# Twenty loads of r and w moved from SP's queue to ScalarE's in a two-phase recurrence and mixing kernel

## The chip, the cores and the metric

The kernel runs on one core of a Trainium2 chip. The metric is the time of one execution on the device, in microseconds (us); each time shown is the median of a few executions. The profile is one further execution, taken by the hardware profiler.

## The reference

Two phases follow each other. The first is a recurrence over 768 steps for 4 batches and 8 heads of width 40, the second mixes its output over tokens and over channels.

```python
for t in range(S):                                   # S = 768, state is [B, H, D, D]
    y[:, :, t] = einsum('bhd,bhde->bhe', rt, state)
    Sa = einsum('bhde,bhe->bhd', state, at)
    state = state * wt[:, :, None, :] - einsum('bhd,bhe->bhde', Sa, bt) \
            + einsum('bhd,bhe->bhde', vt, kt)
x = y.transpose(0, 2, 1, 3).reshape(B, S, H * D)
theta = x @ w_theta
zr, zi = x * cos(theta), x * sin(theta)
u = x + einsum('ts,bsd->btd', w_tok_r, zr) + einsum('ts,bsd->btd', w_tok_i, zi)
out = u + maximum(u @ w_ch, 0)
```

All inputs and the output are float32.

## The kernel before

The 768 steps of a batch are cut into six chunks of 128, so there are 24 tiles (four batches of six), numbered 0 to 23. Within a tile the recurrence is written as matrix products: decays from sums of log w, masked score matrices, a small carried state. A tile needs six inputs of 128 x 8 x 40 floats (160 KB): r, k, v, w, a, b. For r and w one load brings two tiles at once (320 KB), so an even tile's load serves the odd tile behind it as well.

What is done when is written out by hand. The string `ORDER` is a list of some 1,400 entries such as `LDR:4`, `LN:6A` or `PSI:4@1`: a step's name, the tile, for some the engine (A is ScalarE, ACT in the profile; V is VectorE, DVE; G is GpSimd, POOL; S is SyncE, SP) and the PSUM bank. A loop at the end runs through it and calls one function an entry. Each engine gets its instructions in the written order and runs them one after the other, waiting on semaphores where an operand or a buffer is not ready. The entries that this text speaks of:

- `LDW`, `LDR`, `LDK`, `LDB`, `LDA`, `LDV`: the loads of w, r, k, b, a, v (L348, L334, L354 for k and b, L359 for a and v). All are issued by SP's queue. `raw_w` and `raw_r` have three buffers each, the others five.
- `LDT`: a load of rows of a token-mixing weight (`wtok_raw`, L773), also SP's; `ST` stores a tile of the output; a few transposes are SP's DMAs too.
- `LN:i`: ScalarE's logarithm of w for tiles i and i+1 (`lw_two`, L366). The sums, `INVW` (L401) and `WI` (L443) on ScalarE, and `KH` and `AH` on POOL come from it.
- `CR:i`: the cast of r for two tiles (`r`), on ScalarE or POOL.
- ScalarE's many other entries move or cast results out of PSUM (L293), and TensorE's next products wait for these: `EGD` (`gd`), `EPHI` (`phi`), `ERT` (`rvT`), `ETH` (`th`) among them; `SIN` is the sine and cosine with a table load before it (L728).

Each hardware DMA reports its landing on one of eight completion semaphores, `DMAHW0` to `DMAHW7` in the rows below, with 16 for a whole load. The recording layer gives them out in turn, in the order in which it places the DMAs, and a DMA first waits until every earlier one on its semaphore has landed.

Of the kernel before, what the change touches and what calls it, by code (L numbers as in the profile page):

```python
# [19 lines left out]
LDW:2 LDW:0 LDK:0 LDA:1 LDC:0.0G LDC:0.2G LDA:0 LN:0A LDB:0 CSE:0@0 CSI:0@1 LN:2A CST:0 LDB:1  # L20
LDK:1 INVW:0A WI:0A LDK:2 AH:0V CSI:2@1 CSE:2@0 AH:1V KH:0V CST:2 LDB:2 TRA:0@0 TRK:0@3 LDV:0
EAT:0A INVW:2A LDR:0 EKBT:0V LDA:2 WI:2A KH:1V PHI:0@1 EPHI:0A PSI:0@0 LDV:1 KH:2G TRA:1@2
EPSI:0V TRK:1@1 EKBT:1V LDB:3 CV:0A MPHI:0G EAT:1A X0:0@0 TRK:2@3 EKBT:2V LDK:3 ENX:0A CR:0A
PHI:1@1 PSI:1@0 EPHI:1V LDV:2 AH:2G TRV:0@2 EPSI:1A TRR:0@1 NU:0 LDW:4 EVT:0V ENU:0A TRA:2@3
MPSI:1G GT:0@0 CV:1A EAT:2V EGT:0V ERT:0A NUT:0@2 LDR:2 PSI:2@0 ENUT:0A PHI:2@1 EPSI:2A TRV:1@3
EPHI:2V KH:3G X0:1@0 LDA:3 ENX:1A LDB:4 LV:0@0 NU:1 EVT:1A LU:0@1 CV:2G ENU:1A ELV:0V TRK:3@2
MPSI:2G ELU:0A NUT:1@3 LDK:4 ERT:1V GT:1@0 GI:1 ENUT:1V LN:4A LV:1@0 LU:1@1 MLU:0G EGT:1V
TRV:2@1 LDV:3 X0:2@3 CR:2G ELV:1A Y:0@0 ELU:1V ENX:2A CSI:4@0 LDA:4 AH:3G LDB:5 EX:0V CSE:4@1
INVW:4A EKBT:3V CST:4 MLV:1G TRA:3@0 LDK:5 WI:4A TRR:2@2 EAT:3V NU:2 EVT:2A ERT:2V KH:4G PSI:3@0
EPSI:3V PHI:3@1 ENU:2A ERT:3A GD:0@0 GT:2@1 LDR:4 NUT:2@3 EGD:0A GI:2 ENUT:2V EPHI:3A LDW:6  # L30
TRK:4@2 AH:4G EGT:2V LU:2@0 EKBT:4V CV:3A LV:2@1 MPHI:3G LDA:5 X0:3@0 ELU:2A TRA:4@3 Y:1@1
ELV:2V MLU:2G ENX:3A NU:3 EAT:4V TRV:3@2 LDV:4 ENU:3A LDK:6 EX:1V GD:1@3 PHI:4@0 EVT:3V KH:5G
PSI:4@1 EGD:1A GT:3@0 EPSI:4A EPHI:4V NUT:3@1 Y:2@2 CR:4G ENUT:3V LN:6A LV:3@0 LDB:6 EX:2V
LU:3@1 ELU:3V TRK:5@3 MPSI:4G ELV:3A LDA:6 TRR:4@1 ERT:4A AH:5G GI:3 GD:2@2 EGT:3V CSE:6@0 LDV:5
CSI:6@1 EGD:2A EKBT:5V CV:4G INVW:6A TRA:5@0 LDK:7 MLV:3G X0:4@2 ENX:4A ERT:5V CST:6 EAT:5V
TRV:4@3 XT:1@1 LDB:7 WI:6A XT:0@0 EVT:4V NU:4 KH:6G LDR:6 PHI:5@1 EXT:1A EXT:0V PSI:5@0 ENU:4A
EPHI:5V TH:0@3 AH:6G EPSI:5A NUT:4@0 TRK:6@1 ENUT:4V LDW:8 EKBT:6V LV:4@1 MPSI:5G LU:4@0 Y:3@2
LDV:6 LDA:7 SIN:0A CV:5G ELU:4V GT:4@0 GI:4 TRV:5@1 KH:7G EGT:4V ELV:4A EVT:5V MLV:4G TH:1@3
X0:5@0 EX:3V XT:2@1 SIN:1A LDB:8 LV:5@0 TRA:6@2 ENX:5V EXT:2V ELV:5A GD:3@3 EAT:6V TH:2@1 NU:5
CR:6G SIN:2A EGD:3V MLV:5G PSI:6@1 PHI:6@0 LDA:8 ENU:5V EPSI:6V LDV:7 Y:4@2 NUT:5@3 LDK:8  # L40
TRR:6@0 ENUT:5V CV:6G EPHI:6V LN:8A TRK:7@1 X0:6@3 ENX:6A AH:7G LU:5@1 ZR:1G LDB:9 LDK:9 CSE:8@0
ERT:7A ELU:5V NU:6 CST:8 ERT:6A ENU:6A TRA:7@0 ZR:2G EKBT:7V WI:8A AH:8G LDW:10 CSI:8@1 EAT:7V
GD:4@3 INVW:8A TRV:6@1 EX:4V PSI:7@0 PHI:7@1 NUT:6@0 EVT:6V EPSI:7V LDA:9 GT:6@2 KH:8G EGD:4A
Y:5@1 LDV:8 EPHI:7A EGT:6V CV:7A LV:6@0 ENUT:6V MPHI:7G TRA:8@3 EAT:8A EX:5V LDT:0.0 X0:7@2
TRK:8@0 ENX:7V ELV:6A GD:6@1 XT:4@3 EKBT:8V KH:9G NU:7 LDT:0.1 ENU:7A LU:6@1 EXT:4V PSI:8@0
EGD:6V NUT:7@0 EPSI:8V XT:3@3 ELU:6A TRV:7@2 ZR:0G TRK:9@1 ENUT:7A LDV:9 LDR:8 EXT:3V LU:7@1
GT:7@0 AH:9G LN:10A TH:3@3 CV:8G LDK:10 EKBT:9V TH:4@1 ELU:7V GI:7 CW:0.0G PHI:8@0 SIN:3A EVT:7V
LDT:1.0 MLU:6G EGT:7V LV:7@1 SIN:4A TRA:9@2 XT:5@3 EXT:5A X0:8@0 EPHI:8V LDB:10 WT:0.0@1 EAT:9V
CW:0.1G ENX:8A EWT:0.0A ELV:7V TH:5@3 MLV:6G PSI:9@0 EPSI:9V SIN:5A WT:0.1@2 CR:8G NU:8 TRV:8@1
EVT:8V LDT:1.1 ENU:8A LDA:10 Y:7@3 EWT:0.1A CV:9G CSI:10@1 EX:7V PHI:9@0 GT:8@0 LDR:10 ZR:5G  # L50
CW:1.0G NUT:8@2 GI:8 LDV:10 EPHI:9V TRR:8@1 EGT:8V Y:6@3 INVW:10A CSE:10@0 KH:10G LDB:11 CST:10
ENUT:8A ERT:9A LDK:11 EX:6V ERT:8V X0:9@0 WT:1.0@3 WI:10A ENX:9V TRV:9@2 CW:1.1A EWT:1.0V LV:8@1
LU:8@0 AH:10G ELV:8V TRK:10@1 YR:0.0@3 EVT:9A LDT:2.0 ZR:3G NU:9 EKBT:10A CV:10G YR:0.1 TRA:10@2
LDW:12 LV:9@1 ELU:8V ENU:9A YR:0.2 ZR:4G EAT:10A GD:7@1 EGD:7A ELV:9V CR:10A WT:1.1@0 GT:9@2
LDA:11 GI:9 PSI:10@0 EPSI:10A EGT:9V PHI:10@1 EWT:1.1V EPHI:10V LDT:2.1 NUT:9@1 TRR:10@2 Y:8@0
ENUT:9A MPSI:10G ERT:10A TRV:10@1 EX:8V YR:0.3 YR:0.4 LDK:12 EVT:10V X0:10@0 LDB:12 KH:11G
ERT:11V LN:12A ENX:10V LV:10@0 LU:9@1 ELV:10A CW:2.0G YR:0.5 ELU:9V NU:10 LDV:11 TRK:11@1
ENU:10A GD:8@2 CW:2.1A AH:11G EU:0V LDA:12 EKBT:11V CSI:12@0 CSE:12@1 CST:12 LDW:14 TRA:11@0
WT:2.1@3 EAT:11V INVW:12A KH:12G WT:2.0@1 LDK:13 WI:12A LDB:13 PSI:11@0 EWT:2.1A EWT:2.0V
PHI:11@1 XT:6@0 EPSI:11V NUT:10@1 GT:10@3 EGD:8A CV:11A GI:10 Y:9@2 EXT:6A LDT:3.0 AH:12G  # L60
EPHI:11A MPHI:11G TRV:11@0 EGT:10V LDC:0.4G EX:9V TRK:12@3 ENUT:10V EKBT:12V EVT:11A MLV:10G
# [6 lines left out]
ELU:11V ZR:7G CSE:14@0 ERT:12A ERT:13V PSI:13@1 LDV:14 EX:10V CW:3.1A CST:14 TRV:12@2 EVT:12A
EPSI:13V YR:1.4 KH:14G LDR:14 YR:1.5 NU:12 WI:14A GD:10@1 WT:3.1@2 ENU:12V EGD:10A LDK:15
PHI:13@1 LV:12@0 EWT:3.1V GT:12@0 EU:1V CV:13G EPHI:13A NUT:12@1 ENUT:12A AH:14G EGT:12V  # L70
TRV:13@2 ELV:12V Y:11@3 LDB:15 TRK:14@0 EVT:13A MPHI:13G LDT:4.1 YR:3.0@1 EX:11V LV:13@1 ELV:13V
LU:12@0 EKBT:14A ZR:8G UT:0@2 TRA:14@3 EAT:14V X0:13@0 ELU:12A YR:3.1 LDT:4.0 YR:3.2 ENX:13A
YR:3.3 CV:14A CR:14A PHI:14@1 PSI:14@0 EUT:0A MLU:12G TRV:14@3 LDA:15 EPHI:14V YR:3.4 EVT:14A
NU:13 YR:3.5 EU:3V LDW:16 UT:1@2 ENU:13A KH:15G TRR:14@3 EUT:1A CW:4.1G NUT:13@0 ERT:14A CH:0@1
ENUT:13V CHR:1@2 CH:1 EPSI:14A LDV:15 EO:0V Y:12@0 CW:4.0G EO:1V LV:14@1 LU:13@0 ERT:15A EX:12V
ST:1 GD:12@1 EGD:12V XT:9@2 TRK:15@3 EXT:9V EKBT:15V GT:13@0 ELU:13A WT:4.1@1 EWT:4.1V TH:9@2
AH:15G ELV:14A MPSI:14G TRA:15@3 EAT:15V ST:0 MLU:13G GI:13 LDT:5.1 ETH:9A WT:4.0@1 XT:11@2
ZR:6G EGT:13V LN:16A PHI:15@0 EWT:4.0V LDT:5.0 PSI:15@1 X0:14@3 EXT:11V LDK:16 XT:10@0 CV:15G
YR:4.0@1 YR:4.1 ENX:14V TH:11@2 LDB:16 EXT:10V SIN:9A NU:14 EPHI:15V YR:4.2 ETH:11A LDA:16
ENU:14A TH:10@0 CW:5.1G YR:4.3 SIN:10A Y:13@2 EPSI:15V EX:13V GT:14@3 LDK:17 NUT:14@0 SIN:11A  # L80
ZR:10G CSI:16@0 CSE:16@1 EUT:2S EGA:14V EGT:14V CW:5.0G TRV:15@2 YR:4.4 EVT:15V YR:4.5 LDB:17
X0:15@3 ENUT:14V INVW:16A EU:4V CST:16 KH:16G WT:5.1@2 ENX:15V LDW:18 WI:16A WT:5.0@0 EWT:5.1V
LU:14@0 LV:15@1 EWT:5.0V ELV:15V NU:15 LDR:16 XT:12@1 YR:5.0@2 LDV:16 AH:16G YR:5.1 ELU:14A
ENU:15A TRK:16@0 LDA:17 MLU:14G TRA:16@3 EXT:12V EKBT:16V YR:5.2 YR:5.3 EAT:16A NUT:15@1 MLV:14G
UT:3@0 LDK:18 EUT:3V GD:13@3 EGD:13A PHI:16@0 KH:17G PSI:16@1 ENUT:15A EPHI:16V CH:2@0 YR:5.4
# [809 lines left out]
```

## Time and profile before

| | |
|---|---|
| median of 3 runs | 206.38 us (205.11 to 210.47) |
| profiled execution | 205.09 us |
| span from its first to its last instruction | 203.4 us |
| TensorE (PE) busy | 186.8 us, 92% |
| VectorE (DVE) busy | 169.8 us, 83% |
| ScalarE (ACT) busy | 150.1 us, 74% |
| GpSimd (POOL) busy | 148.1 us, 73% |
| hardware DMA queue, share of the 16 DMA engines | 83.9% |

An engine's busy time counts its own instructions; issuing a DMA or waiting on a semaphore is not in it. The 1.7 us between span and execution lie around the span. All sums in the prediction are made against the profiled execution.

### The profile page before, as it was taken

Reading aid. Unit: us, or ns where it says so; the run is one execution under the profiler, and the core shown is the slowest. Engines: PE = TensorE matmul, PEld = TensorE weight load, DVE = VectorE, ACT = ScalarE, POOL = GpSimd, SP = SyncE. Lnnn points to the kernel's source line nnn. Section 1 sums busy time; section 2 is a strip of 40 time slices with the busy share of each in tenths; the row PEclk is TensorE's granted clock in tenths of the full one; section 3 lists DMA queues with packets and bytes.
Section 4 is the critical chain, followed back from the end, with each engine's and each line's share of the span. In section 5 each row is a group of like instructions: output and inputs, shape, how many; then the busy total and the mean of one; then the engine's idle time right before and its main releaser. Section 6 shows DMA issues by size and latency. Waiting matters only on the chain.

```text
span 203.4 us, 7844 instructions
## 1 busy us (share of the span) xinstructions
PE 186.8 (92%) x3282; PEld 147.3 (72%) x3282; DVE 169.8 (83%) x324; ACT 150.1 (74%) x273; POOL 148.1 (73%) x155
## 2 busy tenths in 40 slices
...
GB/s 156 182 192 157 206 173 197 141 212 158 208 269 266 197 248 178 212 238 175 224 270 207 201 175 177 140 207 214 152 164 77 181 190 127 74 75 53 193 77 129
DMA packets 141955, 35.95 MB, mean 177 GB/s; under 512 B 136352, under 2 KB 140384, under 8 KB 141920
## 3 DMA queue, kind: packets, MB, share of 16 engines
q1 hardware_dynamic: 140864, 34.85, 83.9%
...
q14 instruction: 10, 0.08, 0.1%
HBM read 29.54 MB, written 3.93 MB: 165 GB/s over the span
## 4 chain that ended last, share of the span: by engine, by line
PE 68%; DVE 9%; ACT 8%; DMA 8%; POOL 3%; SPq 2%; issue 1%; POOLq 0%; DVEq 0%; ACTq 0%
PE sm L306 35%; PE sc L306 16%; PE sm L310 16%; DMA raw_kb<-in_b_dram 5%; DMA wtok_raw<-in_moe_w_tok_i_dram 3%; POOL kb L303 2%; DVE phi L303 1%; ACT cs L728 1%; DVE lamu L303 1%; DVE rvT L295 1%; SPq L359 1%; ACT rvT L293 1%; DVE kbT L295 1%; DVE u_two L756 1%; DVE oo L765 1%
## 5 line engine op out<-in xcount | busy, mean ns | idle before, releaser
L303 POOL TENSOR_TENSOR kb<-raw_kb,invW_two 128x640 bf16<-128x640 f32 x22 | 34.1, 1552 | 16.4 <-DMA raw_kb<-in_b_dram 9.8
L303 POOL TENSOR_TENSOR z<-cs,x_two 128x640 bf16<-128x640 f32 x22 | 30.8, 1404 | 6.4 <-ACT cs L728 5.6
L306 PE MATMUL sm<-z,wtok_r 128*128 128x320 bf16 x120 | 34.6, 300 | 0.0
L306 PE MATMUL sm<-z,wtok_i 128*128 128x320 bf16 x120 | 34.5, 299 | 0.0
L303 DVE TENSOR_TENSOR phi<-sc,mask_p 128x1024 bf16<-128x1024 f32 x17 | 20.7, 1218 | 2.7 <-PE sc L306 2.5
L303 POOL TENSOR_TENSOR ah<-raw_a,Wi_two 128x320 bf16<-128x320 f32 x22 | 19.0, 865 | 3.3 <-issue 2.2
L303 DVE TENSOR_TENSOR psi<-sc,mask_p 128x1024 bf16<-128x1024 f32 x15 | 18.2, 1216 | 0.6 <-PE sc L306 0.5
L306 PE MATMUL sc<-aT,kbT 64*128 64x128 bf16 x384 | 16.8, 223 | 0.9 <-DVE kbT L295 0.8
L306 PEld LDWEIGHTS <-wtok_i 128*128 128x128 bf16 x144 | 14.1, 98 | 4.5 <-issue 1.3
L306 PEld LDWEIGHTS <-wtok_r 128*128 128x128 bf16 x144 | 14.0, 97 | 4.5 <-issue 0.5
L303 DVE TENSOR_TENSOR lamu<-sc,mask_p 128x1024 bf16<-128x1024 f32 x14 | 17.1, 1218 | 0.3
L310 PE MATMUL sm<-ident,kb 128*128 128x128 bf16 x184 | 15.4, 231 | 1.6 <-DVE kb L303 1.0
L306 PEld LDWEIGHTS <-rvT 64*128 64x128 bf16 (+1 forms) x272 | 13.8, 95 | 3.5 <-issue 1.4
L295 DVE COPY kbT<-sm 128x1024 bf16<-128x1024 bf16 x20 | 13.7, 685 | 2.6 <-PE sm L310 2.5
L306 PEld LDWEIGHTS <-kbT 64*128 64x128 bf16 x384 | 11.6, 97 | 5.7 <-issue 3.4
L585 POOL TENSOR_SCALAR_AFFINE_SELECT lamv<-lamv 128x1024 bf16<-128x1024 bf16 x13 | 14.2, 1093 | 1.2 <-ACT lamv L293 1.2
L306 PE MATMUL sm<-kb,lamv 128*128 128x40 bf16 x192 | 15.0, 180 | 0.0
L306 PE MATMUL sm<-kb,lamu 128*128 128x40 bf16 x192 | 14.9, 179 | 0.0
L310 PEld LDWEIGHTS <-kb 128*128 128x128 bf16 x184 | 11.9, 104 | 3.0 <-DVE kb L303 1.3
L293 ACT CAST lamv<-sc 128x1024 bf16<-128x1024 f32 x13 | 13.1, 1010 | 1.1 <-PE sc L306 1.0
L303 DVE TENSOR_TENSOR lamv<-sc,mask_p 128x1024 bf16<-128x1024 f32 x11 | 13.4, 1218 | 0.4 <-PE sc L306 0.4
L306 PE MATMUL sm<-wth,xT 128*128 128x320 bf16 x72 | 13.7, 299 | 0.0
...
## 6 DMA issues: line engine op xcount, KB each, us to landing
...
raw_kb<-in_k_dram SPq DMA_DIRECT2D x24, 160.0 KB, 4.2
raw_a<-in_a_dram SPq DMA_DIRECT2D x24, 160.0 KB, 4.3
raw_kb<-in_b_dram SPq DMA_DIRECT2D x24, 160.0 KB, 4.3
raw_v<-in_v_dram SPq DMA_DIRECT2D x24, 160.0 KB, 4.6
...
out_dram<-oo SPq DMA_DIRECT2D x24, 160.0 KB, 2.0
wtok_raw<-in_moe_w_tok_r_dram SPq DMA_DIRECT2D x6, 384.0 KB, 4.8
```

The source lines that it names most:

```text
L293: keep(nc.scalar.copy(out=out, in_=in_))
L295: keep(eng[e].tensor_copy(out=out, in_=in_))
L303: keep(eng[e].tensor_tensor(out=out, in0=in0, in1=in1, op=ALU.mult))
L306: keep(nc.tensor.matmul(out, lhsT=lhsT, rhs=rhs, start=start, stop=stop, skip_group_check=True))
L310: keep(nc.tensor.transpose(out=out, in_=in_, identity=ident))
L359: keep(nc.sync.dma_start(out=t, in_=source(ap, i)))
L585: keep(nc.gpsimd.affine_select(out=flat, in_=flat, compare_op=ALU.is_ge, fill=0.0, base=-1, pattern=[[0, 2 * G], [1, 128]], channel_multip ...
L728: keep(nc.scalar.activation(out=cs[i % 5][:, c], in_=tiles[i].theta, func=AF.Sin, bias=(math.pi / 2, 0.0)[c]))
L756: keep(nc.vector.tensor_tensor(out=q.u, in0=q.rps, in1=q.x, op=ALU.add))
L765: keep(nc.vector.scalar_tensor_tensor(out=q.oo, in0=q.ops[:, 0:DM], scalar=0.0, in1=q.u, op0=ALU.max, op1=ALU.add))
```

## The change

Twenty entries get an `A`: `LDW` of the tiles 4, 6, ..., 22 and `LDR` of the tiles 2, 4, ..., 20. They stay where they stand in `ORDER`. `LDW:0`, `LDW:2`, `LDR:0` and `LDR:22` and all other loads stay on SP's queue.

```diff
+    def queue(e):
+        return nc.scalar if e == "A" else nc.sync
+
-    def load_r(i):
+    def load_r(i, e):
...
-        keep(nc.sync.dma_start(
+        keep(queue(e).dma_start(
             out=tiles[i].raw_r,
             in_=two_of(r, i)))
...
-    def load_w(i):
+    def load_w(i, e):
...
             t = tile_of(raw_w, [128, H, 2 * D], FP32, "raw_w_two")
-            keep(nc.sync.dma_start(out=t, in_=two_of(w, i)))
+            keep(queue(e).dma_start(out=t, in_=two_of(w, i)))
...
-        "LDW": lambda i, j, e, b: load_w(i), "LDK": lambda i, j, e, b: load_kb(k, 0, i),
+        "LDW": lambda i, j, e, b: load_w(i, e), "LDK": lambda i, j, e, b: load_kb(k, 0, i, e),
...
```

In `ORDER` itself, one of the twenty (the others read alike):

```diff
-EPSI:0V TRK:1@1 EKBT:1V LDB:3 ... NU:0 LDW:4 EVT:0V ENU:0A ... ERT:0A NUT:0@2 LDR:2 PSI:2@0
+EPSI:0V TRK:1@1 EKBT:1V LDB:3 ... NU:0 LDW:4A EVT:0V ENU:0A ... ERT:0A NUT:0@2 LDR:2A PSI:2@0
```

What the built programs hold at three places follows. A row gives the source line, the operation, what it writes and reads, and the semaphores that it waits for. Numbers behind a name tell buffers and uses apart: `raw_r_two_728` is `LDR:4`, `raw_w_two_742` is `LDW:6`, `raw_v_840` is `LDV:4`, `raw_v_976` is `LDV:5`, `raw_r_two_1052` is `LDR:6`, `raw_w_two_1102` is `LDW:8`, `raw_kb_1346` holds `LDB:9` and then `LDK:9`, `raw_r_two_2383` is `LDR:12`, `raw_kb_2436` begins with `LDB:14`. In the changed program a line's number is lower by 2 (by 5 for L293 and L295).

First place, ACT's line around `LDR:4` and `LDW:6`, before:

```order
L293 COPY rvT_712<-sm2_668 128x512 [waits DVE_49,Activation_49]
L293 CAST gd_735<-sm0_714 128x320 [waits PE_49]
L293 CAST phi_740<-sc1_702 128x1024
L293 CAST v_3_106<-raw_v_591 128x8x40 [waits DMAHW6_49]
L293 CAST lamu_792<-sc0_755 128x1024 [waits PE_49,Pool_49]
```

and in the change:

```order
L288 COPY rvT_712<-sm2_668 128x512 [waits DVE_49,Activation_49]
L332 DMA raw_r_two_728<-in_r_dram 128x8x80 [waits DMAHW3_49]
L288 CAST gd_735<-sm0_714 128x320 [waits PE_49]
L288 CAST phi_740<-sc1_702 128x1024
L346 DMA raw_w_two_742<-in_w_dram 128x8x80 [waits DMAHW7_49]
L288 CAST v_3_106<-raw_v_591 128x8x40 [waits DMAHW5_49]
L288 CAST lamu_792<-sc0_755 128x1024 [waits PE_49,Pool_49]
```

Both loads now stand in ACT's line, each with a wait of its own, and the instructions behind them come after it. SP's line at the same place, before:

```order
L334 DMA raw_r_two_728<-in_r_dram 128x8x80 [waits DMAHW2_49]
L348 DMA raw_w_two_742<-in_w_dram 128x8x80 [waits DMAHW3_49,Activation_49]
L359 DMA raw_a_777<-in_a_dram 128x8x40 [waits DMAHW4_49]
L359 DMA raw_v_840<-in_v_dram 128x8x40 [waits DMAHW5_49]
L354 DMA raw_kb_843<-in_k_dram 128x8x40 [waits DMAHW6_49,Pool_49]
L354 DMA raw_kb_843<-in_b_dram 128x8x40 [waits DMAHW7_49]
L359 DMA raw_a_950<-in_a_dram 128x8x40 [waits DMAHW0_49]
L359 DMA raw_v_976<-in_v_dram 128x8x40 [waits DMAHW1_49,Activation_49]
```

and in the change:

```order
L357 DMA raw_a_777<-in_a_dram 128x8x40 [waits DMAHW2_49]
L357 DMA raw_v_840<-in_v_dram 128x8x40 [waits DMAHW3_49]
L352 DMA raw_kb_843<-in_k_dram 128x8x40 [waits DMAHW4_49,Pool_49]
L352 DMA raw_kb_843<-in_b_dram 128x8x40 [waits DMAHW5_49]
L357 DMA raw_a_950<-in_a_dram 128x8x40 [waits DMAHW6_49]
L357 DMA raw_v_976<-in_v_dram 128x8x40 [waits DMAHW7_49,Activation_49]
```

The two loads are gone from SP's line, and the loads behind them moved up. The semaphores were given out anew. On `DMAHW3` stand, in this order, `raw_a_214`, `raw_r_two_294`, `raw_kb_500`, `raw_v_840` and then ACT's `raw_r_two_728`: its wait in the program is for 64, four loads of 16, so it goes out after `LDV:4` has landed, which was behind it before. ACT's `raw_w_two_742` waits on `DMAHW7` for 64 in the same way, that is for `raw_v_976`, `LDV:5`.

Second place, ACT's line around `LDR:6` and `LDW:8`, before:

```order
L552 ACTIVATE nx_1011<-sm2_998 128x320 [waits PE_49]
L443 ACTIVATE Wi_two_1036<-sc0_971 128x656 [waits DVE_49,PE_49]
L293 COPY xT_1063<-sm1_1031 128x192 [waits PE_49]
L552 ACTIVATE nu_0_107<-sm2_998 128x8x40 [waits PE_49]
L293 CAST psi_1084<-sc0_1067 128x1024 [waits PE_49]
```

and in the change:

```order
L550 ACTIVATE nx_1011<-sm2_998 128x320 [waits PE_49]
L441 ACTIVATE Wi_two_1036<-sc0_971 128x656 [waits DVE_49,PE_49]
L332 DMA raw_r_two_1052<-in_r_dram 128x8x80 [waits DMAHW2_49]
L288 COPY xT_1063<-sm1_1031 128x192 [waits PE_49]
L550 ACTIVATE nu_0_107<-sm2_998 128x8x40 [waits PE_49]
L288 CAST psi_1084<-sc0_1067 128x1024 [waits PE_49]
L346 DMA raw_w_two_1102<-in_w_dram 128x8x80 [waits DMAHW3_49]
```

and SP's line in the change from the next loads to those that these two wait for:

```order
L357 DMA raw_v_1146<-in_v_dram 128x8x40 [waits DMAHW2_49,Pool_49]
L357 DMA raw_a_1148<-in_a_dram 128x8x40 [waits DMAHW4_49]
L352 DMA raw_kb_1200<-in_b_dram 128x8x40 [waits DMAHW5_49]
L357 DMA raw_a_1265<-in_a_dram 128x8x40 [waits DMAHW6_49,Pool_49]
L357 DMA raw_v_1270<-in_v_dram 128x8x40 [waits DMAHW0_49,Activation_49]
L352 DMA raw_kb_1200<-in_k_dram 128x8x40 [waits DMAHW1_49]
L352 DMA raw_kb_1346<-in_b_dram 128x8x40 [waits DMAHW2_49,Pool_49]
L352 DMA raw_kb_1346<-in_k_dram 128x8x40 [waits DMAHW3_49]
```

`LDR:6` now waits on `DMAHW2` for 96, whose last 16 come from the first load into `raw_kb_1346` (`LDB:9`), and `LDW:8` on `DMAHW3` for 96, whose last come from the second (`LDK:9`). Both were ahead of all the rows above on SP's line.

Third place, ACT's line around `LDR:12`, before:

```order
L293 COPY xT_2355<-sm1_2331 128x192 [waits PE_49]
L366 ACTIVATE lw_two_1_94<-raw_w_two_2189 128x16x40 [waits DMAHW6_49]
L293 COPY th_192<-sm0_2357 128x320 [waits PE_49]
L728 ACT_TABLE_LOAD
L728 ACTIVATE cs_1_194<-th_192 128x320 [waits Activation_49]
```

and in the change:

```order
L288 COPY xT_2355<-sm1_2331 128x192 [waits PE_49]
L364 ACTIVATE lw_two_1_94<-raw_w_two_2189 128x16x40 [waits DMAHW3_49]
L288 COPY th_192<-sm0_2357 128x320 [waits PE_49]
L332 DMA raw_r_two_2383<-in_r_dram 128x8x80 [waits DMAHW4_49]
L726 ACT_TABLE_LOAD
L726 ACTIVATE cs_1_194<-th_192 128x320 [waits Activation_49]
```

`LDR:12` waits on `DMAHW4` for 160, whose last 16 come from the first load into `raw_kb_2436` (`LDB:14`), the load right behind it on SP's line before.

Of the other moved loads, `LDW:4` waits for nothing, and the rest wait in the same way for a load of SP's that stands nearer in the written order or ahead of them.

More of the change, by code (lines that the diff above doesn't have):

```diff
@@ L19 @@
 ORDER = """
[L20 to L61, printed above, removed]
@@ L68 @@
[L68 to L85, printed above, removed]
@@ L110 @@
-YR:11.2 CV:21G UT:9@3 EUT:9A YR:11.3 CH:8@1 EGA:20V EGT:20V CSI:22@0 EUT:10S CHR:9@3 ZR:16G
+LDW:2 LDW:0 LDK:0 LDA:1 LDC:0.0G LDC:0.2G LDA:0 LN:0A LDB:0 CSE:0@0 CSI:0@1 LN:2A CST:0 LDB:1 LDK:1
+INVW:0A WI:0A LDK:2 AH:0V CSI:2@1 CSE:2@0 AH:1V KH:0V CST:2 LDB:2 TRA:0@0 TRK:0@3 LDV:0 EAT:0A
+INVW:2A LDR:0 EKBT:0V LDA:2 WI:2A KH:1V PHI:0@1 EPHI:0A PSI:0@0 LDV:1 KH:2G TRA:1@2 EPSI:0V TRK:1@1
+EKBT:1V LDB:3 CV:0A MPHI:0G EAT:1A X0:0@0 TRK:2@3 EKBT:2V LDK:3 ENX:0A CR:0A PHI:1@1 PSI:1@0 EPHI:1V
+LDV:2 AH:2G TRV:0@2 EPSI:1A TRR:0@1 NU:0 LDW:4A EVT:0V ENU:0A TRA:2@3 MPSI:1G GT:0@0 CV:1A EAT:2V
@@ new lines @@
+EGT:0V ERT:0A NUT:0@2 LDR:2A PSI:2@0 ENUT:0A PHI:2@1 EPSI:2A TRV:1@3 EPHI:2V KH:3G X0:1@0 LDA:3
+ENX:1A LDB:4 LV:0@0 NU:1 EVT:1A LU:0@1 CV:2G ENU:1A ELV:0V TRK:3@2 MPSI:2G ELU:0A NUT:1@3 LDK:4
+ERT:1V GT:1@0 GI:1 ENUT:1V LN:4A LV:1@0 LU:1@1 MLU:0G EGT:1V TRV:2@1 LDV:3 X0:2@3 CR:2G ELV:1A Y:0@0
+ELU:1V ENX:2A CSI:4@0 LDA:4 AH:3G LDB:5 EX:0V CSE:4@1 INVW:4A EKBT:3V CST:4 MLV:1G TRA:3@0 LDK:5
+WI:4A TRR:2@2 EAT:3V NU:2 EVT:2A ERT:2V KH:4G PSI:3@0 EPSI:3V PHI:3@1 ENU:2A ERT:3A GD:0@0 GT:2@1
+LDR:4A NUT:2@3 EGD:0A GI:2 ENUT:2V EPHI:3A LDW:6A TRK:4@2 AH:4G EGT:2V LU:2@0 EKBT:4V CV:3A LV:2@1
@@ new lines @@
+MPHI:3G LDA:5 X0:3@0 ELU:2A TRA:4@3 Y:1@1 ELV:2V MLU:2G ENX:3A NU:3 EAT:4V TRV:3@2 LDV:4 ENU:3A
+LDK:6 EX:1V GD:1@3 PHI:4@0 EVT:3V KH:5G PSI:4@1 EGD:1A GT:3@0 EPSI:4A EPHI:4V NUT:3@1 Y:2@2 CR:4G
+ENUT:3V LN:6A LV:3@0 LDB:6 EX:2V LU:3@1 ELU:3V TRK:5@3 MPSI:4G ELV:3A LDA:6 TRR:4@1 ERT:4A AH:5G
+GI:3 GD:2@2 EGT:3V CSE:6@0 LDV:5 CSI:6@1 EGD:2A EKBT:5V CV:4G INVW:6A TRA:5@0 LDK:7 MLV:3G X0:4@2
+ENX:4A ERT:5V CST:6 EAT:5V TRV:4@3 XT:1@1 LDB:7 WI:6A XT:0@0 EVT:4V NU:4 KH:6G LDR:6A PHI:5@1 EXT:1A
+EXT:0V PSI:5@0 ENU:4A EPHI:5V TH:0@3 AH:6G EPSI:5A NUT:4@0 TRK:6@1 ENUT:4V LDW:8A EKBT:6V LV:4@1
```

155 lines of the change are left out of this document (97 added, 58 removed).

## Prediction

> **What bounds the kernel now.** I read the page first, then the windows view (a stretch, its us, then busy us and instructions of PE, PEld, DVE, ACT and POOL, then the granted clock, the DMA engines' share and GB/s).
>
> ```profile
> span 203.4 us, 7844 instructions
> PE 186.8 (92%) x3282; PEld 147.3 (72%) x3282; DVE 169.8 (83%) x324; ACT 150.1 (74%) x273; POOL 148.1 (73%) x155
> ...
> q1 hardware_dynamic: 140864, 34.85, 83.9%
> ```
> ```profile
> 17.00:31.00 14.00, 13.33 (x287) 10.80 (x286) 12.76 (x20) 12.72 (x23) 11.62 (x12) 1.00 0.95 181
> 31.00:46.00 15.00, 14.39 (x316) 11.88 (x314) 13.97 (x26) 13.33 (x24) 13.90 (x15) 1.00 0.92 181
> 17.00:100.00 83.00, 79.92 (x1640) 64.84 (x1639) 78.07 (x123) 73.69 (x135) 73.66 (x76) 1.00 0.98 201
> 126.00:160.00 34.00, 34.00 (x611) 26.85 (x610) 30.20 (x56) 29.02 (x52) 28.50 (x29) 1.00 0.82 165
> ```
>
> Two things are full at once. TensorE is busy 79.9 of 83 us between 17 and 100, and all of 126 to 160, so a stretch in which it stands still is hardly won back. And from 17 to 100 the DMA engines are busy 0.98 of the time. So SP's line of loads moves at the pace of the engines, 201 GB/s: 0.8 us for a load of 160 KB, 1.6 us for one of 320 KB. SP's timeline (start us, us, the load) shows the same from the other side: a row begins as soon as the one before it ends.
>
> ```profile
> 28.18 0.84 SPq L334 DMA_DIRECT2D raw_r_two<-in_r_dram  x1
> 29.12 0.68 SPq L348 DMA_DIRECT2D raw_w_two<-in_w_dram  x1
> 29.84 1.10 SPq L359 DMA_DIRECT2D raw_a<-in_a_dram  x1
> 30.99 2.13 SPq L359 DMA_DIRECT2D raw_v<-in_v_dram  x1
> ...
> 35.61 2.43 SPq L359 DMA_DIRECT2D raw_v<-in_v_dram  x1
> ...
> 48.56 1.52 SPq L354 DMA_DIRECT2D raw_kb<-in_b_dram  x1
> 50.12 0.71 SPq L354 DMA_DIRECT2D raw_kb<-in_k_dram  x1
> ```
>
> These are `LDR:4`, `LDW:6`, `LDA:5`, `LDV:4`, then `LDV:5`, `LDB:9` and `LDK:9`. ScalarE's timeline tells where it is meanwhile:
>
> ```profile
> 28.39 0.58 ACT L293 COPY rvT<-sm 128x512 bf16<-128x512 bf16 x1
> 28.87 0.43 ACT L293 CAST gd<-sm 128x320 bf16<-128x320 f32 x1
> 29.19 1.03 ACT L293 CAST phi<-sc 128x1024 bf16<-128x1024 f32 x1
> 30.09 0.48 ACT L293 CAST v<-raw_v 128x320 bf16<-128x320 f32 x1
> ...
> 34.50 0.74 ACT L366 ACTIVATE lw_two<-raw_w_two 128x640 bf16<-128x640 f32 x1 [0.27 <-DMA raw_w_two<-in_w_dram]
> ```
>
> `LDR:4` comes right behind the `rvT` copy, `LDW:6` right behind `phi`. ScalarE is there at 29.0 and 30.2, and SP issued the two loads at 28.2 and 29.1. The two lines run level in the written order: loads land just as they are needed (`LN:6` waited 0.27 us for its own).
>
> **The change part by part.** Moving the issue by itself is nearly neutral: the same bytes on the same engines, from an engine that comes to the entry within about 1 us of SP. What weighs is the wait that each moved load carries. By the rows of the built program, `LDR:4` on ScalarE waits until `LDV:4` has landed, and `LDW:6` until `LDV:5` has: loads of SP's that stand three and six loads further on. While ScalarE waits there, everything behind it in its line waits too: `gd`, `phi`, `psi`, `LN:6`, `invW`, which TensorE's next products read, and POOL's `KH` and `AH`. The landings, from the tile view of single loads:
>
> ```profile
> L359 SPq DMA_DIRECT2D raw_v<-in_v_dram x1: 2131/2131/2131, 31.0 to 31.0; - x1
> ...
> DMA to landing us min/median/max: 4.7/4.7/4.7
> ```
> ```profile
> L359 SPq DMA_DIRECT2D raw_v<-in_v_dram x1: 2431/2431/2431, 35.6 to 35.6; - x1
> ...
> DMA to landing us min/median/max: 4.8/4.8/4.8
> ```
>
> Step 1, `LDR:4`. `LDV:4` landed at 31.0 + 4.7 = 35.7. In the change `LDR:4` and `LDW:6` are no longer ahead of it, 3.2 us of transfer: 32.5. ScalarE is there at 29.0 and waits 3.5. Behind a wait the issue itself isn't covered by other work; SP's issues of these loads bound it:
>
> ```profile
> L348 SPq DMA_DIRECT2D raw_w_two<-in_w_dram x12: 387/576/2437, 0.8 to 142.7; - x12
> L334 SPq DMA_DIRECT2D raw_r_two<-in_r_dram x12: 581/814/1793, 11.8 to 156.3; - x12
> ```
>
> I take 0.6, since ScalarE's queue is empty where SP's is full; 0.4 to 2.4 are the ends. `gd` and `phi` follow, 1.2 us (28.87 to 30.09): ScalarE is at `LDW:6` at 34.3.
>
> Step 2, `LDW:6`. `LDV:5` landed at 40.4; without `LDW:6` ahead of it, 38.8. Wait 4.5, issue 0.6: ScalarE goes on at 39.4 where it was at 30.1, 9.3 us late.
>
> Step 3, `LDR:6` and `LDW:8`, which wait for `LDB:9` and `LDK:9`.
>
> ```profile
> 37.97 0.71 ACT L443 ACTIVATE Wi_two<-sc 128x656 f32<-128x656 f32 x1
> ...
> 39.36 1.01 ACT L293 CAST psi<-sc 128x1024 bf16<-128x1024 f32 x1
> ```
>
> The tile view of the loads at 48.56 and at 50.12:
>
> ```profile
> DMA to landing us min/median/max: 3.9/3.9/3.9
> ```
> ```profile
> DMA to landing us min/median/max: 3.4/3.4/3.4
> ```
>
> `LDB:9` landed at 48.6 + 3.9 = 52.5; two moved loads less, 49.3. ScalarE reaches `LDR:6` at 38.7 + 9.3 = 48.0: wait 1.3, issue 0.6. `LDK:9` landed at 50.1 + 3.4 = 53.5, less one load 51.9; ScalarE is at `LDW:8` at 40.4 + 11.2 = 51.6: 0.3 and 0.6. It is now 12.1 late, and SP's line is that much ahead of it. The engines were idle for 0.05 of 14 us and 0.08 of 15, 1.9 in all; a line with two queues behind it may close these gaps, so between 0 and 1.9 come off. I take 1.5: 10.6.
>
> Step 4, `LDR:12`. SP's lead does not last: at 59.4 it waits for POOL, which is late like the others, and its queue runs empty.
>
> ```profile
> 59.42 0.91 SPq L773 DMA_DIRECT2D wtok_raw<-in_moe_w_tok_r_dram  x1
> 82.10 0.42 ACT L293 COPY th<-sm 128x320 f32<-128x320 f32 x1
> 84.99 1.38 SPq L354 DMA_DIRECT2D raw_kb<-in_b_dram  x1
> ```
>
> SP's own waits (for whom, us in total, times, longest), and the landing of the load at 84.99 in the tile view:
>
> ```profile
> SPq L773 <- POOL wtok_row L295: 0.3, 1, 0.3
> ```
> ```profile
> DMA to landing us min/median/max: 4.5/4.5/4.5
> ```
>
> From there both lines are equally late. `LDB:14` landed at 85.0 + 4.5 = 89.5, less `LDR:12` 87.9; ScalarE is there at 82.5: 5.4 us if the lines keep level, nothing if SP is ahead by as much. An empty queue gives it a lead; the page has the ends of a flight:
>
> ```profile
> out_dram<-oo SPq DMA_DIRECT2D x24, 160.0 KB, 2.0
> wtok_raw<-in_moe_w_tok_r_dram SPq DMA_DIRECT2D x6, 384.0 KB, 4.8
> ```
>
> 4.8 in a full queue against 2.0 late in the kernel, 2.8 of lead. I take 2.6: 13.2.
>
> Step 5, the other 15 issues. ScalarE's rows overlap by 0.1 (`phi` starts at 29.19, `gd` ends at 29.30), so its sequencer works on the next instruction while one runs; an issue of 0.6 behind an instruction of 0.4 to 1.0 costs 0 to 0.2. I take 0.1 each, 1.5 in all (0 and 0.8 each are the ends): 14.7.
>
> Step 6, what comes back: TensorE's 3.1 us of idle time between 17 and 100 can be used up: 11.6. The sum is 205.1 (the profiled execution, 203.4 of span and 1.7 around it) + 11.6 = **216.7 us**. The median of the runs, 206.4, lies 1.3 above the profiled execution; I keep to the latter.
>
> [...]
>
> **The rivals.** *Issues are dear on ScalarE.* The two medians make 5.8 + 8.1 = 13.9 us for the twenty; my sum has 4.5 of it. ScalarE's idle 9.3 us of 83 take up half of the other 9.4: 221.4. For it: SP's longest issues; against: SP's queue was full, ScalarE's is not.
>
> *SP's line moves up faster.* If SP's issuing sets its pace rather than the engines, each moved issue brings the rest forward by its own length.
>
> ```profile
> 17.45 2.44 SPq L348 DMA_DIRECT2D raw_w_two<-in_w_dram  x1
> 19.93 0.69 SPq L334 DMA_DIRECT2D raw_r_two<-in_r_dram  x1
> ```
>
> These two and the rows at 28.18 and 29.12 make 4.7: `LDV:4` lands at 31.0, the wait is 2.0, `LDV:5` at 35.7, the wait then 2.9; 6.1 late with both issues, and about 7.5 after step 3. Less 3.1: 209.5. Against it: the share of 0.98.
>
> *No difference.* If SP is so far ahead that no wait is felt, SP saves time that it spent on full engines, and ScalarE's issues hide: 205.1. [...]
>
> *Faster.* The chain that ended last runs through loads twice in this stretch:
>
> ```profile
> 34.27 4.63 DMA raw_kb<-in_b_dram
> ```
> ```profile
> 86.47 5.80 DMA wtok_raw<-in_moe_w_tok_i_dram
> ```
>
> Ahead of each stood one moved load on SP's line (`LDW:6`, `LDR:12`). Without these each ends 1.6 earlier: 201.9. It decides only if `LDV:4` has landed by 29.0 and `LDV:5` by 30.2, over 3 and 8 us earlier than my sum has them.
>
> **How the numbers follow.** Forecast 0.62, dear issues 0.17, SP's line faster 0.09, no difference 0.07, faster 0.05. About 2% can be told from no change; half of the 209.5 case lies within it. So slower by over 2%: 0.62 + 0.17 + 0.045, 0.84; within 2%: 0.11; faster: 0.05. The range is 207.5 to 225.0: below, steps 1 and 2 with all that may come off (9.3 - 1.9 - 3.1 = 4.3, 209.4) and most of the faster line; above, step 4 at 5.4 and the dear issues (216.7 + 2.8 + 4.7 = 224.2).
>
> **What would show it.** Right: ScalarE idle for 2 us or more before `gd` behind the `rvT` copy and again before the `v` cast behind `phi` near 30 to 40 us, TensorE and POOL idle there too, more space than today between `LDV:5`'s landing and its use, a wait of 1 to 5 us before the table load behind `LDR:12`, and hardly any loss after 100. Wrong: no idle time of ScalarE over 1 us at these places, or ScalarE slowed evenly at all twenty issues (the dear ones).

## The result and the profile after

The change takes 220.75 us (median of 4 runs, 219.31 to 221.23) where the kernel before takes 206.51 (205.11 to 210.47): a ratio of 1.070, 95% interval 1.062 to 1.079. The profiled execution of the change took 221.17 us with a span of 219.4, against 205.1 and 203.4. Of two kernels further down (the early waits with TensorE kept busy) the profiled execution was a disturbed one, over 400 us; their times are those of their other executions, and no line of their traces is used.

The page of the change, in the lines that answer to those of before:

```profile
span 219.4 us, 7837 instructions
PE 192.4 (88%) x3282; PEld 152.2 (69%) x3282; DVE 170.8 (78%) x324; ACT 150.8 (69%) x273; POOL 148.4 (68%) x155
...
PE   0679961999999998938999999999999999999892
...
PEclk9999995599999999995999999999999999999998
DMA  7999999999126999999193999999676778332523
```

The same instructions take the same time within 1 us on every engine but TensorE (186.8 before, 192.4 now); what has grown is idle time. It stands in two places, the sixth and seventh slice (27 to 38 us) and the 18th and 19th (93 to 104 us), and some way behind each the DMA engines run empty for some slices (`126`, `193`): SP has gone ahead and then waits for buffers that late engines still hold (longest 17.0 us, for POOL's `wtok_row`). The clock row, all nines before but for the last slice, has fives at the end of each.

ScalarE's timeline (start us, us, engine, line, instruction; in brackets the idle time before it and what ended it; ACTq are its issues) at the places that the prediction named:

```profile
29.45 0.59 ACT L288 COPY rvT<-sm 128x512 bf16<-128x512 bf16 x1
31.35 0.37 ACTq L332 DMA_DIRECT2D raw_r_two<-in_r_dram  x1
31.76 0.43 ACT L288 CAST gd<-sm 128x320 bf16<-128x320 f32 x1 [1.73 <-DMA raw_v<-in_v_dram]
32.09 1.02 ACT L288 CAST phi<-sc 128x1024 bf16<-128x1024 f32 x1
37.31 0.37 ACTq L346 DMA_DIRECT2D raw_w_two<-in_w_dram  x1
37.72 0.46 ACT L288 CAST v<-raw_v 128x320 bf16<-128x320 f32 x1 [4.62 <-DMA raw_v<-in_v_dram]
...
85.91 0.37 ACTq L346 DMA_DIRECT2D raw_w_two<-in_w_dram  x1
86.33 0.70 ACT L399 ACTIVATE invW_two<-sc 128x640 f32<-128x640 f32 x1 [0.93 <-PE sm L305]
...
96.52 0.38 ACTq L332 DMA_DIRECT2D raw_r_two<-in_r_dram  x1
96.92 1.28 ACT L726 ACT_TABLE_LOAD   x1 [4.59 <-DMA raw_kb<-in_b_dram]
```

`gd` and the `v` cast need neither `LDV:4` nor `LDV:5` here; they stand behind `LDR:4` and `LDW:6`, whose issues wait for those loads. The chain of work that ended last (start us, us, what; its `issue` pieces of 0.02 and 0.04 us are left out here) runs through exactly these waits:

```profile
28.01 3.32 DMA raw_v<-in_v_dram
31.35 0.37 ACTq L332
31.76 0.01 ACT gd L288
31.77 5.51 DMA raw_v<-in_v_dram
37.31 0.37 ACTq L346
...
89.99 6.50 DMA raw_kb<-in_b_dram
96.52 0.38 ACTq L332
```

`v` starts at 37.72 where it started at 30.09: 7.6 us late. The table load starts at 96.92 instead of 82.54, 14.4 late; the span is 16.0 longer. ScalarE was 1.1 us late already before the first of these waits: the `rvT` copy in front of it started at 29.45 instead of 28.39. TensorE's products between 17 and 20 us had taken longer than before, though the clock row has nines there; the first kernel's row, then the change's:

```profile
17.22 0.79 PE L306 MATMUL sc<-aT,kbT 64*128 64x128 bf16 x16
```
```profile
17.34 1.04 PE L301 MATMUL sc<-aT,kbT 64*128 64x128 bf16 x16
```

This differs from one execution to the next. Two kernels further down that are alike up to there (the late waits, without and with TensorE kept busy) have that copy at 27.93 and 29.44. So I count this 1.1 us to the execution, not to the change.

TensorE's timeline has the same stalls one step on:

```profile
33.16 0.40 PE L301 MATMUL sc<-rvT 64*128 64x128 bf16 x8 [1.88 <-ACT phi L288]
38.23 0.23 PE L301 MATMUL sm<-v,psi 128*128 128x40 bf16 x2 [4.54 <-ACT v L288]
...
99.43 0.61 PE L305 MATMUL sm<-ident,nu 128*128 128x128 bf16 x4 [3.99 <-ACT nu L550]
```

And one thing that no step of the prediction had, in the windows view (columns as in the prediction; the third from the right is the granted clock):

```profile
31.00:33.60 2.60, 0.72 (x17) 0.49 (x14) 0.83 (x3) 1.34 (x2) 0.42 (x1) 1.00 1.02 185
33.70:43.80 10.10, 5.57 (x99) 5.22 (x98) 4.11 (x6) 4.22 (x7) 4.48 (x5) 0.50 1.12 193
44.00:46.00 2.00, 2.00 (x43) 1.72 (x39) 1.92 (x3) 1.53 (x3) 2.00 (x4) 1.00 1.11 189
...
98.50:105.30 6.80, 5.87 (x53) 4.40 (x54) 1.88 (x4) 5.94 (x13) 2.60 (x3) 0.50 0.94 158
```

For 10 us in and behind the early stalls and for 7 us behind the last, TensorE runs at half its clock (0.50 granted), also after the wait is over.

### The profile page after: what moved, and what is told of

Its sections match the earlier page's. It is cut to its first block, busy times and chain, and to the rows that moved or that the text cites. A ratio compares the mean times of both kernels' runs of the same rounds, so it can differ in the third digit from the quotient of the medians.

```text
span 219.4 us, 7837 instructions
## 1 busy us (share of the span) xinstructions
PE 192.4 (88%) x3282; PEld 152.2 (69%) x3282; DVE 170.8 (78%) x324; ACT 150.8 (69%) x273; POOL 148.4 (68%) x155
## 4 chain that ended last, share of the span: by engine, by line
PE 58%; DMA 12%; SPq 9%; DVE 8%; ACT 4%; POOL 4%; issue 3%; ACTq 1%; DVEq 0%; POOLq 0%
PE sm L301 30%; PE sc L301 14%; PE sm L305 14%; DMA raw_kb<-in_b_dram 6%; SPq L352 4%; DMA raw_v<-in_v_dram 4%; SPq L357 4%; DMA raw_kb<-in_k_dram 2%; DVE phi L298 1%; DVE lamu L298 1%; DVE rvT L290 1%; ACT nu L550 1%; POOL wtok_row L290 1%; DVE kbT L290 1%; ACT rvT L288 1%
## 5 line engine op out<-in xcount | busy, mean ns | idle before, releaser
L301 PE MATMUL sc<-aT,kbT 64*128 64x128 bf16 x384 | 17.6, 229 | 1.5 <-DVE kbT L290 0.8
L301 PEld LDWEIGHTS <-wtok_i 128*128 128x128 bf16 x144 | 14.2, 98 | 4.5 <-issue 1.3
L301 PEld LDWEIGHTS <-kbT 64*128 64x128 bf16 x384 | 12.2, 99 | 6.5 <-issue 4.0
L583 POOL TENSOR_SCALAR_AFFINE_SELECT lamu<-lamu 128x1024 bf16<-128x1024 bf16 x10 | 10.9, 1093 | 7.7 <-ACT lamu L288 7.7
L301 PE MATMUL sm<-kb,lamv 128*128 128x40 bf16 x192 | 15.5, 183 | 0.0
L301 PE MATMUL sm<-v,psi 128*128 128x40 bf16 x192 | 11.1, 184 | 4.5 <-ACT v L288 4.5
L583 POOL TENSOR_SCALAR_AFFINE_SELECT lamv<-lamv 128x1024 bf16<-128x1024 bf16 x13 | 14.2, 1092 | 1.1 <-ACT lamv L288 1.0
L288 ACT CAST lamv<-sc 128x1024 bf16<-128x1024 f32 x13 | 13.2, 1013 | 1.9 <-PE sc L301 1.5
```

Source lines behind the costliest of these rows:

```text
L288: keep(nc.scalar.copy(out=out, in_=in_))
L301: keep(nc.tensor.matmul(out, lhsT=lhsT, rhs=rhs, start=start, stop=stop, skip_group_check=True))
L583: keep(nc.gpsimd.affine_select(out=flat, in_=flat, compare_op=ALU.is_ge, fill=0.0, base=-1, pattern=[[0, 2 * G], [1, 128]], channel_multip ...
```

## The experiments

**The same instructions, other waits.** In the built program of the change ScalarE's loads are placed far behind SP's, so the load that had the semaphore before, eight places back, is one that SP issues later in the written order. The trace shows that wait: by the chain above `LDV:4` landed at 31.33, and the issue of `LDR:4` started at 31.35. An edge from each moved load to SP's next one in the written order, which orders the layout and puts no semaphore in the program, makes it follow the written order:

```diff
+    def written(e, ins):
+        keep(ins)
+        if e == "A":
+            last_act[0] = ins
+        elif last_act[0] is not None:
+            tc.add_manual_dep(
+                ins.ins, last_act[0].ins.name,
+                mybir.DependencyInfo(mybir.DependencyClass.NoSync, mybir.DependencyReason.DATA),
+                reason="written order")
+            last_act[0] = None
...
-            keep(queue(e).dma_start(out=t, in_=two_of(w, i)))
+            written(e, queue(e).dma_start(out=t, in_=two_of(w, i)))
```

> The instructions of every engine stand in the same order as in the change, all twenty loads are still issued by ScalarE; only which earlier load each one waits for differs: it is now a load eight places back in the written order, which has long landed (LDR:4 waits for LDR:2, LDW:6 for LDA:4). My theory (the waits on loads further on cost the time): the ScalarE waits before gd and before v near 30 to 38 us and before the table load behind LDR:12 go, TensorE's clock stays at 1.0, and the time is that of the kernel before, 205 to 208 us. Rival, dear issues on ScalarE: all twenty issues are still there, 217 to 222. Rival, two queues on full DMA engines cost by themselves: between, 210 to 216.

Measured: 206.17 us (10 runs, 204.94 to 207.08), ratio to the kernel before 1.0005, interval 0.997 to 1.004. All twenty issues are still on ScalarE, and the loss is gone. Its ScalarE timeline and its loads of w by queue (ns min/median/max, first and last start):

```profile
28.42 0.59 ACT L288 COPY rvT<-sm 128x512 bf16<-128x512 bf16 x1
28.45 0.38 ACTq L345 DMA_DIRECT2D raw_r_two<-in_r_dram  x1
28.91 0.43 ACT L288 CAST gd<-sm 128x320 bf16<-128x320 f32 x1
28.91 0.55 ACTq L359 DMA_DIRECT2D raw_w_two<-in_w_dram  x1
29.22 1.03 ACT L288 CAST phi<-sc 128x1024 bf16<-128x1024 f32 x1
30.13 0.48 ACT L288 CAST v<-raw_v 128x320 bf16<-128x320 f32 x1
```
```profile
L359 ACTq DMA_DIRECT2D raw_w_two<-in_w_dram x10: 374/375/546, 17.9 to 143.4; - x10
```

The issue of `LDR:4` starts while the `rvT` copy in front of it runs and is over before the copy is; `v` starts at 30.13, 0.04 us later than before. One load landed later (`lw_two` behind `LDW:6` starts at 35.31, not 34.50), and by the table load at 46.41 the two kernels are level again. So here an issue that waits for nothing cost ScalarE nothing that shows (0.04 us at `v`), two queues on full engines (DMA share 1.05 from 17 to 100 us) cost nothing that can be measured in the time (ratio 1.0005), and the whole loss of the change is in which loads its issues wait for.

**The early and the late waits apart.** The same kernel, with the edge left out for the first nine moved loads (then these keep the change's waits, the later ones do not), or for `LDW:14`, `LDR:12`, `LDR:14` and `LDW:16` (the other way about):

```diff
-            last_act[0] = ins
+            last_act[0] = None if now[0] in LEFT_OUT else ins
```

`LEFT_OUT` stands here for the list of those loads, `now` for the entry at hand.

> As the first kernel of this set, but the first nine moved loads keep the waits of the change (LDR:4 for LDV:4, LDW:6 for LDV:5, LDR:6 for LDB:9, LDW:8 for LDK:9); from LDW:12 on the waits are for loads long landed. My theory: the early stall alone, ScalarE 8.5 to 9 us late from 45 us on as in the change, no stall behind LDR:12: 213 to 216 us. Rival, dear issues: as the change, 219 to 222.

> As the first kernel of this set, but LDW:14, LDR:12, LDR:14 and LDW:16 keep the waits of the change (LDR:12 for LDB:14, LDR:14 for LDK:14, LDW:16 for LDK:15); the early ones wait for loads long landed. My theory: nothing is lost up to 80 us, then one stall of about 5 us before the table load behind LDR:12 (LDB:14 landed at 89.5 when the two lines ran level, 87.9 with LDR:12 not ahead of it, ScalarE there at 82.5) and a stretch of half clock after it: 210 to 214 us. Early and late loss together make that of the change, 14 to 16. Rival, dear issues: as the change, 219 to 222. Rival, the late stall only exists because the early one upset the lines: 205 to 208.

Measured: 213.36 us, 1.036 (1.031 to 1.041), and 213.07 us, 1.032 (1.025 to 1.038). Each has its own stall and not the other's. The two losses, 7.1 and 6.8 us, make 13.9, against 14.2 in the change. The second kernel, measured once more, took 211.89 us, 6.1 more than the kernel before. The late stall does not need the early one: with the lines level at 82 us it was 6.4 us in one execution and 4.4 in another, beside 4.6 in the change (ScalarE's own waits in the first of them: for whom, us, times, longest):

```profile
ACT L739 <- DMA raw_kb<-in_b_dram: 6.4, 1, 6.4
```

**ScalarE held up by nothing but itself.** The kernel before, all loads on SP:

```diff
+    def hold(times):
+        for n in range(times):
+            keep(nc.scalar.copy(out=spare, in_=ident))
...
-LDR:4 ... LDW:6
+LDR:4 HOLD:9 ... LDW:6 HOLD:24
```

> The kernel before, all loads on SP, with 33 copies of the identity (128 x 128) on ScalarE that nobody reads: 9 at the place of LDR:4, 24 at that of LDW:6, by estimate 1.7 and 4.6 us of ScalarE's time. My theory: ScalarE's lateness at these places is what costs, whatever it comes from, at about one us of the total for each us there: 211 to 214. Rival, the loss needs the loads to leave SP's line (SP running ahead, engines empty later): 205 to 208. The copies' own times, which their rows will show, set the price: the time lost should be that of the copies, within 1.5 us.

Measured: 216.10 us, 1.050 (1.043 to 1.058). My estimate of 0.19 us for a copy was too low; the copies took:

```profile
28.40 2.94 ACT L294 COPY spare<-ident 128x128 bf16<-128x128 bf16 x9
32.47 7.88 ACT L294 COPY spare<-ident 128x128 bf16<-128x128 bf16 x24
40.26 0.45 ACT L298 CAST v<-raw_v 128x320 bf16<-128x320 f32 x1
```

`v` is 10.2 us late and the kernel loses 9.2 by the medians, 10.3 by the ratio. So a microsecond of ScalarE at this place is worth about one of the whole, whether it waits or works, and such a loss does not need a load to have left SP's line.

**Fewer loads moved, other waits.** The change with only `LDR:4`, `LDW:6`, `LDW:14` and `LDR:12` moved, and with `LDR:12` alone (the letter A taken off the others):

> LDR:4, LDW:6, LDW:14 and LDR:12 alone are issued by ScalarE. With four moved, LDR:4 waits for LDB:4 and LDW:6 for LDB:5 (both landed by 30.0), LDW:14 for LDB:12 (78.1), LDR:12 for LDA:13, which stands right ahead of it on SP's line and landed at 87.2; ScalarE was there at 82.5. My theory: no early stall, one of about 4.7 us behind LDR:12: 209.5 to 212. Rival, these four loads cost by their place or by the move: as the change, 217 to 221. Rival, an issue's price only: 206 to 207.5.

> LDR:12 alone is issued by ScalarE; it waits for the load at 79.74 (wtok_raw), which landed at 85.2 where ScalarE was there at 82.5. My theory: a stall of 2.6 us, 207.5 to 209.5. With the wait of 4.7 us in the kernel with four moved and of 6.4 in the one with the late waits (213.1), the loss should rise by about one us for each us waited. Rival, the stall costs nothing until it is over some length: 205 to 207.

Measured: 210.29 us, 1.021 (1.014 to 1.029), and 207.77, 1.012 (1.003 to 1.021). ScalarE's waits in the first kernel and in the second:

```profile
ACT L726 <- DMA raw_a<-in_a_dram: 2.2, 1, 2.2
...
ACT invW_two L399 <- PE sm L305: 1.3, 1, 1.3
```
```profile
ACT L726 <- DMA wtok_raw<-in_moe_w_tok_r_dram: 2.8, 1, 2.8
```

`LDR:4` and `LDW:6` are moved here too and cost nothing: their waits are for loads that have landed. `LDR:12` waits for `LDA:13` in one and for the `wtok_raw` load in the other, as expected. In the first `LDW:14` waits for `LDB:12`, which I had named without counting it: it costs the 1.3 us before `invW_two`, so ScalarE comes later to `LDR:12` and waits 2.2 there, not 4.7. Its table load starts 5.0 us late, the other kernel's 2.5. The same load moved, late by 2.5, 5.0 and 7.4 us (the late waits alone), loses 2.5, 4.4 and 6.5 us by the ratios. In these executions 0.2, 0.8 and 0.1 us of the lateness were already there at the `rvT` copy of 28.39.

**The half clock.** TensorE was kept busy through the stalls with products of the identity that the next product overwrites:

```diff
+    def busy(out, times):
+        for n in range(times):
+            mm(out, ident, ident, True, True)
```

First in the whole change, at all three places (at the late one with transposes of the identity):

> The change with 171 more products of the identity on TensorE, 56 ns each, at the three places where TensorE stands still in the change (30 before LU:2, 75 before X0:3, 66 before NUT:11); they write where the next product overwrites. The waits stay, only TensorE isn't idle in them. My theory: the granted clock stays near 1.0 where it was 0.5 for 10.2 and 6.8 us, and 2 to 3.5 us of the loss go: 217 to 219 us. Rival, the half clock costs nothing because TensorE waits for others there anyway: 220 to 222. Rival, the clock drops for another reason than idleness: clock still 0.5 in those stretches, 220 to 224.

Measured: 224.29 us (221.82 to 227.65), 1.084 (1.077 to 1.090), slower than the change. The 56 ns show in its trace: 30 products took 1.84 us and 75 took 4.36, 2.52 for the 45 more. The late products were put in the wrong place: their bank comes free only when the stall is over, so that they ran behind it, at half clock:

```profile
100.41 6.55 PE L309 MATMUL sm<-ident 128*128 128x128 bf16 x66 [3.12 <-ACT nu L557]
```

The time of that kernel decides nothing. So early and late apart. Early, on the kernel with the early waits alone, twice:

> The kernel with the early waits alone (213.4 us, clock 0.5 for 6.8 us), with 125 products of the identity more on TensorE, 56 ns each, where it stands still (50 before LU:2, 75 before X0:3). The granted clock should stay at 1.0 between 30 and 45 us. If the half clock is a part of the loss: 210.5 to 212.5. If it isn't, because what sets the pace there is ScalarE's lateness and the engines that wait for it: 212.5 to 215. After the kernel with 171 such products, whose ScalarE was 9.5 us late at 44 us with the clock at 1.0 against 8.9 in the change, I lean to the second.

> The kernel with the early waits alone (213.4 us), with 105 products of the identity (5.9 us of TensorE's 7.0 idle; 40 before LU:2, 65 before X0:3), so that none outlasts the wait. Clock 1.0 from 30 to 45 us. If the half clock is a part of the early loss: 210.5 to 212.5. If not, as the 125 products suggested: 213 to 215.

Measured: 213.9 to 215.5 us, 1.043 (1.036 to 1.049), and 214.2 to 215.4, 1.043 (1.036 to 1.050), beside 1.036 without the products. The mean clock of these runs was 0.989 to 1.000 against 0.967 to 0.984, so the half clock was all but gone, and nothing was won. There is no trace that shows where these products ran, so it is not excluded that they took as much as they won.

Late, with the products ahead of `YR:1.0`, the last work that TensorE has before it stands still:

> The kernel with the late waits alone (213.1 us; TensorE idle 5.8 us before NUT:11, then clock 0.5 for 6.8 us), with 95 products of the identity (56 ns each, 5.3 us) on TensorE ahead of YR:1.0, the last work it has before it stands still. The clock should stay at 1.0. In the kernels with short stalls behind LDR:12, where the clock stayed at 1.0, ScalarE made up 1.1 to 1.7 us within 12 us; in this one it fell back by a further 1.3 under the half clock. If the half clock is a part of the loss: 1.5 to 3 us less than without these products, 210 to 211.5. If not: 212.5 to 214.5.

> The kernel with the late waits alone once more, beside the one with TensorE kept busy: 212.5 to 214, 3.2% over the kernel before, by both readings.

> The change (220.8 us) with 66 products of the identity (3.7 of 4.0 us idle) on TensorE ahead of YR:1.0, to keep the clock up in the late stall alone. If the half clock after the late stall is a part of the loss: 217.5 to 219.5. If not: 220 to 222.

Measured: 211.24 us, 1.025 (1.020 to 1.031), against 211.89, 1.029 (1.023 to 1.034), for the same kernel without the products: by the times not told apart. The change with them: 218.43 us, 1.058 (1.050 to 1.065), where the change has 1.070 (1.062 to 1.079); that is 2.3 us by the medians, with intervals that just overlap. The windows of the change and of that kernel:

```profile
91.00:116.00 25.00, 20.52 (x329) 15.79 (x324) 16.96 (x25) 16.60 (x34) 16.27 (x18) 0.86 0.82 167
```
```profile
91.00:116.00 25.00, 24.55 (x449) 20.38 (x448) 19.41 (x30) 18.78 (x37) 19.22 (x21) 1.00 0.90 186
```

The traces tell more than the times, because each starts from its own wait: the time from the table load behind `LDR:12` to `Wi_two`, before, in the change, and in the change with TensorE busy:

```profile
82.54 1.28 ACT L728 ACT_TABLE_LOAD   x1
...
112.26 0.72 ACT L443 ACTIVATE Wi_two<-sc 128x656 f32<-128x656 f32 x1
```
```profile
128.07 0.72 ACT L441 ACTIVATE Wi_two<-sc 128x656 f32<-128x656 f32 x1
```
```profile
97.03 1.28 ACT L730 ACT_TABLE_LOAD   x1 [3.93 <-DMA raw_kb<-in_b_dram]
...
125.89 0.72 ACT L445 ACTIVATE Wi_two<-sc 128x656 f32<-128x656 f32 x1
```

29.7 us before; 31.2 in the change; 28.9 with TensorE busy. In the other kernels that stall there it is 30.4 and 31.0 with the half clock (the late waits, two executions), 29.0 and 28.9 without it (the late waits with TensorE busy, `LDR:12` alone). Only kernels that stall there may be compared in this way, because without the stall the stretch also waits for loads: the kernel in written order takes 31.2 us for it at full clock, with this gap of TensorE's in it:

```profile
90.29 0.40 PE L305 MATMUL sm<-ident,ah 128*128 128x128 bf16 x4 [1.88 <-POOL ah L298]
```

So after the late stall the half clock costs 1.4 to 2.3 us; in the change, the chain of work that ended last is TensorE's own from 99.4 to 106.8, without a gap.

After the early stall no cost shows in the time, though ScalarE does lose there: in the change `psi` starts 4.3 us behind the `v` cast, before 3.1. In the kernel with the early waits alone, to which the early products were added, the chain of work that ended last does not touch TensorE from 28.0 to 58.5 us. It runs through POOL and then through `LDR:6`, whose wait for `LDB:9` ends last there:

```profile
42.60 5.01 DMA raw_kb<-in_b_dram
...
47.62 0.39 ACTq L345
```

So what the clock gives back, this wait takes. The kernel with all three places filled, which had the full clock at the early stall, agrees in one execution: `psi` is again 3.1 us behind `v`, then ScalarE stands 1.5 us at `LDR:6`, and the `nu` behind it starts 10.4 us after `v`, in the change 10.6. In the change itself, where that wait costs nothing, the early products were not tried by themselves.

## Why the prediction was right, and where its sum was off

The cause was right: with other loads to wait for, the same issues cost nothing. That ScalarE itself stands while a load of its own waits, on which steps 1 to 4 rest, the change shows: it was idle for 1.73, 4.62 and 4.59 us, issue included, ahead of `gd`, `v` and the table load. The direction and the range held. The sum was short by 4.5 us (216.7 against 221.2 for the profiled execution). Of this, up to 1.1 is the late start of that execution; by the medians the change lost 14.2 us, 2.6 more than the 11.6 of the sum. By its own steps, in ScalarE's lateness:

- **Step 1**, `LDR:4`: a wait and issue of 1.7 us where I had 3.5 and 0.6. `LDV:4` landed at 31.3, not 32.5, and ScalarE came at 30.0, not 29.0 (the late start).
- **Step 2**, `LDW:6`: 4.6 with the issue, against 4.5 and 0.6. `v` 7.6 late instead of 9.3, the late start included.
- **Step 3**, `LDR:6` and `LDW:8`: no wait at all (1.6 foretold). Yet at the `psi` of 39.36, now 48.81, ScalarE was 9.5 late: it had lost 1.8 since `v`, with TensorE at half clock for the first 6 us. At 52 us it was 8.9 late, not 10.6: steps 1 to 3 were 1.7 too dear, and without the late start 2.8.
- **Step 4**, `LDR:12`: 4.6 instead of 2.6, and 0.9 before `invW_two` behind `LDW:14`, which I had at nothing. This is the larger error: from 52 us to the table load ScalarE fell back by 5.5, not 2.6. That the table load came 14.4 late where I had 13.2, and 13.3 without the late start, is luck: steps 1 to 3 were too dear by what step 4 was too cheap. SP's lead was there, larger than I had it: it issued `LDB:14` 5.0 us later than before while ScalarE came 9.8 later. But I took the 4.5 us of before from issue to landing, less 1.6 for one load, and it was 6.5.
- **Step 5**, fifteen issues at 0.1: nothing. They hide behind the instruction that runs, 0.37 to 0.55 each. With that the rival of dear issues falls, and the 0.6 behind a wait was 0.4. (There I said that the sum held 4.5 us of issues; step 4 has none in it, so it held 3.9.)
- **Step 6**, the give-back of 3.1: this is the step that failed. Most of TensorE's idle time of before is not slack that a late line can use up. In the 38 us behind the early stall TensorE was busy 37.04, before in a stretch of that length 36.52 to 37.12:

```profile
46.00:84.00 38.00, 37.04 (x774) 29.93 (x771) 37.50 (x63) 34.51 (x63) 35.19 (x36) 1.00 0.74 167
```
```profile
38.00:76.00 38.00, 36.52 (x758) 29.50 (x757) 36.93 (x61) 34.11 (x62) 35.73 (x37) 1.00 1.00 215
46.00:84.00 38.00, 37.12 (x767) 30.25 (x760) 37.07 (x58) 34.17 (x64) 34.84 (x36) 1.00 1.01 219
```

The DMA share fell from 1.00 to 0.74 there, the loads came early, and TensorE was no faster: what holds it up is, by my reading of these rows, the engines around it (VectorE was busy 37.50 of the 38 us). What did come back is 0.6 us between that `psi` (9.5 late) and 52 us (8.9), and from the table load on 0.7 to 0.9 can (28.9 and 29.0 against 29.7 above); there the half clock, **a term that the sum lacked**, took more than that away. From the table load to the end the change lost another 1.6 where I had it win 1.6; with the 1.2 by which the table load came later than in the sum that is the difference of 4.5, within rounding.

The other rivals: *SP's line moves up faster* is out by its time (209.5), though a part of it was so: `LDV:4` landed at 31.3, near its 31.0 and not my 32.5, and `LDV:5` at 37.3, between its 35.7 and my 38.8. *No difference* is what the kernel in written order shows (206.2 against 206.3 us). What the issues wait for decided this change. *Faster* needed these two landings by 29.0 and 30.2.
